# A Mamba-2 scan fused with a feed-forward layer: B and C turned by VectorE in place of TensorE

## The chip, the cores and the metric

The kernel runs on one core of a Trainium2 chip. A core has five engines that each work through a queue of their own, in order: TensorE (PE in the profile; its weight loads, PEld, overlap its matmuls), VectorE (DVE), ScalarE (ACT), GpSimd (POOL) and SyncE (SP), which here issues nearly all DMA transfers. They wait for one another through semaphores. The metric is the device time of one execution in microseconds; less is better.

## What is computed

The reference first runs a state-space scan over a batch of 4 with 8 heads, 768 tokens, 32 channels and a state of 16. It works in chunks; for each chunk

```python
cum = np.cumsum(la, axis=-1)                       # la = log(a)
L = np.exp(cum[:, :, :, None] - cum[:, :, None, :]) * causal
CB = np.einsum('bhin,bhjn->bhij', Cc, Bc)          # scores
y_intra = np.einsum('bhij,bhjd->bhid', CB * L, xc)
y_inter = np.einsum('bhin,bhnd->bhid', Cc, state) * np.exp(cum)[:, :, :, None]
y[:, :, sl] = y_intra + y_inter
state = decay_full * state + sum_j(Bc[j] * xc[j] * decay_from_j)
```

and then a feed-forward layer on the 3072 x 256 result: `h = x @ w_in` (2048 wide), `g = elu(h)`, `out = g @ w_out`.

## The kernel before

**Blocks.** The 768 tokens of each batch entry are three blocks of 256, which gives 12 blocks, numbered 0 to 11 in the order in which they are worked on. A block has u = 0, 1 (halves of 128 tokens), each of v = 0, 1 (chunks of 64 tokens). Blocks 0 to 3 are handled one by one; from block 4 on they go in pairs (4, 5), (6, 7), (8, 9), (10, 11).

**What a block needs.** `load_bc` brings B and C, `load_x` brings x, `spread_cum` and `spread_exp` bring decays back from DRAM. In `load_bc` tokens lie on the partitions, and each DMA moves rows of 16 floats (64 bytes), one for each token and head. The scores are products over the state index, so B and C must lie with (head, state) on the partitions and tokens along the free dimension: they have to be turned. `turn` does this with four 128x128 transposes on TensorE (L374) into two PSUM tiles `ps_tb` and `ps_tc`. ScalarE copies the turned B into `bt` (L378). VectorE makes `ctm` from the turned C (L381): two copies of it, each with every other head masked out by `hmask2`. `turn_exp` makes `cts` (L389), C times the decay `ec`. `scaled` (L364) makes `sc`, B times a decay, from B as it was loaded, on GpSimd.

Then `scores` (L459, on TensorE) multiplies `bt` and `ctm`; `decay` and `decay_of` fill `L` by exponentials on ScalarE (L439) and cut it to the causal part on GpSimd (L444, once for each half of the heads and each chunk parity); `weigh` (L468, VectorE) multiplies scores and `L` into `M`; `sums`, `states` and `across` (L489, L504 to L511, L534) carry the state on; `inside` (L553) makes the block's output and ScalarE moves it to `yT`, the input of the feed-forward layer.

**The feed-forward layer** is most of TensorE's work. For blocks 0 to 3 it is `l1` (L583) and `l2` (L707), with `elu` between them: on ScalarE a negated relu (L596) and an exponential (L603), on VectorE the combination `g` (L605). For later pairs a scheme with fewer products and more additions is used, in rounds i = 0 to 7: `front`, `mid` and `back` (L655) make the first layer, with `p_copy` on ScalarE (L665) and `u_sum` and further sums on VectorE (L673, L674, L682, L689, L690); `second` makes the second layer (L759), with sums on VectorE and GpSimd (L750, L723, L727). In a round, `mid` writes over a PSUM half that `p_copy` has read, and the first product of `back` needs the sum of L682.

**Weights** come in 16 pieces of float64 words that are rounded to float32 on chip (L157 to L200, on ScalarE, VectorE and GpSimd) while the first blocks are worked on.

**Order.** The program turns automatic scheduling off: every engine executes in the order in which the Python code issues its instructions. Blocks 4 to 11 are prepared by `scan_ahead`, which is called at every half round and gives the turn of the pair's first block after half round 5 and of the second after half round 7. Scores follow in half round 9. Blocks 2 and 3 are turned by explicit calls, block 2 at step 5 of the twelve-step loop (its scores at step 7), block 3 in round 1 of `n == 2` (its scores in round 2). The DMA queue of SyncE is in order as well.

Of the kernel before, what the change touches and what calls it, by code (L numbers as in the profile page):

```python
# [10 lines left out]
F32 = mybir.dt.float32  # L11
U32 = mybir.dt.uint32
BF16 = mybir.dt.bfloat16
ALU = mybir.AluOpType
ACT = mybir.ActivationFunctionType

P = 128
Q = 64
BLK = 2 * P
# [9 lines left out]
def kernel(  # L29
# [27 lines left out]
    nc = tc.nc  # L57
    NB, NH, S, D = x.shape
    N = B.shape[-1]
# [4 lines left out]
    DM, DF = moe_w_in.shape  # L64
# [6 lines left out]
    raw = ctx.enter_context(tc.tile_pool(name="raw", bufs=3))  # L71
    att = ctx.enter_context(tc.tile_pool(name="att", bufs=2))
    ffn = ctx.enter_context(tc.tile_pool(name="ffn", bufs=2))
# [13 lines left out]
    for k in range(4):  # L87
        (nc.scalar if k % 2 else nc.sync).dma_start(
            out=la0[BH * k:BH * (k + 1)],
            in_=a.rearrange("b h (c s) -> (b h) c s", s=P)[:, 0:2, :])  # L90
# [5 lines left out]
    st = {}  # L96

    def place(n):

        return 2 * (n // (2 * NG)) + n % 2, n // 2 % NG  # L100
# [5 lines left out]
    def load_bc(n, c_queue=nc.sync):  # L106
        b, g = place(n)
        st.setdefault(n, {})["bc"] = raw.tile([P, 2, 2, NH, N], F32, tag="bc", name="bc", bufs=2)
        for u in range(2):
            sl = slice((2 * g + u) * P, (2 * g + u + 1) * P)  # L110
            for k, src in enumerate((B, C)):
                (nc.sync, c_queue)[k].dma_start(  # L112
                    out=st[n]["bc"][:, k, u], in_=src[b, :, sl, :].rearrange("h s n -> s h n"))
# [118 lines left out]
    for v in range(2):  # L232
        nc.gpsimd.affine_select(
            out=low16[Q * v:Q * v + Q], in_=low16[Q * v:Q * v + Q], pattern=[[1, Q]],
# [5 lines left out]
        out=hmask, in_=hmask, pattern=[[-N, NH]], compare_op=ALU.is_ge, fill=0.0,  # L240
        base=0, channel_multiplier=1)
    nc.gpsimd.affine_select(
        out=hmask, in_=hmask, pattern=[[N, NH]], compare_op=ALU.is_ge, fill=0.0,
# [3 lines left out]
    hmask2 = const.tile([P, 2], F32, name="hmask2")  # L247
# [4 lines left out]
        out=minus, in0=ident, scalar1=-1.0, scalar2=None, op0=ALU.mult)  # L252
# [106 lines left out]
    def scaled(n, eng):  # L359

        s = st[n]
        s["sc"] = sc = att.tile([P, 2, NH, N], F32, tag="sc", name="sc", bufs=3)
        factor = eb0[:, :, NH * n:NH * (n + 1)] if n < 2 else eb[:, :, rows_of(n)]
        eng.tensor_tensor(  # L364
            out=sc, in0=s["bc"][:, 0],
            in1=factor.unsqueeze(3).to_broadcast([P, 2, NH, N]), op=ALU.mult)

    def turn(n):

        s = st[n]  # L370
        tb, tc_ = psum([P, 2, P], "ps_tb"), psum([P, 2, P], "ps_tc")
        for k, ps in enumerate((tb, tc_)):
            for u in range(2):
                nc.tensor.transpose(  # L374
                    out=ps[:, u], in_=s["bc"][:, k, u].rearrange("p h n -> p (h n)"),
                    identity=ident)
        s["bt"] = att.tile([P, 2, P], F32, tag="bt", name="bt", bufs=3)
        nc.scalar.copy(out=s["bt"], in_=tb)  # L378
        s["ct"] = tc_
        s["ctm"] = att.tile([P, 2, 2, P], F32, tag="ctm", name="ctm")  # L380
        nc.vector.tensor_tensor(  # L381
            out=s["ctm"], in0=tc_.unsqueeze(2).to_broadcast([P, 2, 2, P]),
            in1=hmask2.unsqueeze(1).unsqueeze(3).to_broadcast([P, 2, 2, P]), op=ALU.mult)

    def turn_exp(n):

        s = st[n]
        s["cts"] = att.tile([P, 2, P], F32, tag="cts", name="cts", bufs=3)
        nc.vector.tensor_tensor(out=s["cts"], in0=s.pop("ct"), in1=s["ec"], op=ALU.mult)  # L389

# [307 lines left out]
    def l2(n, j, half=None):  # L700


        if j == 0 and half != 1:
            o_of[n] = p_o.tile([P, 2, DM], F32, tag="o", name="ps_o")
        for m in (2 * j, 2 * j + 1) if half is None else (2 * j + half,):
            for ts in range(2):
                nc.tensor.matmul(  # L707
                    out=o_of[n][:, ts], lhsT=g_of[n, j][:, m % 2, ts * P:(ts + 1) * P],
                    rhs=w_out[:, m], start=(m == 0 and ts == 0), stop=(m == MC - 1),
                    skip_group_check=True)  # L710
        if j == MC // 2 - 1 and half != 0:
            ob = ffn.tile([P, 2, DM], F32, tag="ob", name="ob")
            nc.scalar.copy(out=ob, in_=o_of.pop(n))
            r0 = row_of(n)
            nc.sync.dma_start(
                out=out[r0:r0 + BLK, :].rearrange("(t p) e -> p t e", p=P), in_=ob)
# [197 lines left out]
    for s, (n, i) in enumerate((  # L914
            (1, 0), (1, 1), (1, 2), (0, 4), (1, 3), (0, 5), (1, 4), (0, 6), (1, 5), (0, 7),
            (1, 6), (1, 7))):
        l1(n, i)
        if s < 8:
            decay_of(2, s)
        if s == 7:  # L920
            scores(2)
            weigh(2, 0)
            weigh(2, 1)
        if s % 2 == 1 and todo < 10:
            w_take(todo, nc.vector)
            w_give(todo)
            w_load(todo + 6)
            todo += 1
        if s == 4:
            scaled(2, nc.gpsimd)  # L930
        if s == 5:
            turn(2)
            first_exp(2)
            turn_exp(2)
        if s == 8:
            spread_cum(3)
            load_x(3)
            spread_exp(3)
            weigh(2, 2)
            weigh(2, 3)  # L940

            st[0] = kept
            sums(2, 0, pool=p_o, tag="o", parts=(None, last))
            states(0, last)
            st.pop(0)
            states(2)
        if s == 10:
            spread_cum(4)
            inside(across(2), 2)
        if len(lag) > 1:  # L950
            elu()
# [15 lines left out]
    def scan_ahead(n, i):  # L967


        m = n + 2 + n % 2  # L970
        if 4 < m < NP and n % 2 == 1 and i in (4, 5):
            spread_cum(m + i - 4)
        m = n + 2 - n % 2
        if 4 <= m < NP and n % 2 == 0:
            if i < 2:
                load_bc(m + i)
                spread_exp(m + i)
            if i == 2:
                if m == 4:
                    spread_cum(5)  # L980
                load_x(m)
                load_x(m + 1)
            for k in (i,) if m == 4 else (i, i + 1) if i % 2 == 0 else ():
                if k >= 2:
                    decay(m + k // 6, (k - 2) % 4)
            if i in (5, 7):
                turn(m + i // 7)
                turn_exp(m + i // 7)
        if 4 <= m < NP and n % 2 == 1:
            if i == 0:  # L990
                scaled(m, nc.gpsimd)
                scaled(m + 1, nc.gpsimd)
            for k in (i,) if m == 4 else (i, i + 1) if i % 2 == 0 else ():
                if k < 2:
                    decay(m + 1, k + 2)
            if i == 2 and m == 4:
                scores(m, m + 1)
                sums(m, m + 1)
                for q in range(4):
                    weigh(m, q)  # L1000
                    weigh(m + 1, q)
                states(m)
                states(m + 1)
# [7 lines left out]
    for n in (2, 3):  # L1011
        for i in range(8):
            l2(n - 2, i)
            if todo < len(pieces):
                w_take(todo, nc.vector)
            end_of_two(n, 2 * i)
            l1(n, i)
            if todo < len(pieces):
                w_give(todo)
                w_load(todo + 6)  # L1020
                todo += 1
            while lag:
                elu()
            if n == 2:
                if i < 2:
                    decay(3, 2 * i)
                    decay(3, 2 * i + 1)
                if i == 1:
                    scaled(3, nc.gpsimd)
                    turn(3)  # L1030
                    turn_exp(3)
                if i == 2:
                    scores(3)
                    for q in range(4):
                        weigh(3, q)
                if i == 4:
                    sums(3)
                    states(3)
                if i == 6:
                    inside(across(3), 3)  # L1040
            else:
                if i == 0:
                    s_in[:], s_out[:] = weight_sums(), weight_sums()
                elif i < 7:
                    more_sums(i - 1)
            scan_ahead(n, i)
            end_of_two(n, 2 * i + 1)
    sum_t2(2, 0)
    left = (step for i in (6, 7) for step in weight_steps(nc.vector, a_out, s_out, i))

    for n in range(4, NP, 2):
        m = n + 2 if n + 2 < NP else None
# [13 lines left out]
        for k in range(16):  # L1066
            i = k // 2
# [54 lines left out]
    n = NP - 2  # L1122
# [41 lines left out]
```

## Time and profile before

| what | value |
|---|---|
| time, median of 3 (lowest, highest) | 364.5 us (363.97, 365.75) |
| span of the profiled execution | 362.9 us |
| transposes of B and C on PE (L374) | 48, mean of one 275 and 273 ns |
| bt on ACT (L378), 12 | mean 358 ns |
| ctm on DVE (L381), 12 | mean 682 ns |
| cts on DVE (L389), 12 | mean 414 ns |
| packets of DMA, of these under 512 B | 96,239, 77,312 |

A mean duration is from an instruction's start to its end; instructions of one engine overlap at their edges, so what one costs its engine is rather the distance to the start of the next. "Idle before" of an engine counts only for the engine that sets the end of a stretch. The chain of waits follows the last instruction back to what released it, step by step; in it one sees which engine that is.

### The profile page before, as it was taken

The page shows a single profiled execution, that of the slowest core. Times are in us where ns is not written, and L with a number is a line of the kernel's source. Part 1 is how long each engine was busy: PE and PEld are TensorE (multiplying, and loading weights), DVE is VectorE, ACT ScalarE, POOL GpSimd, SP SyncE. Part 2 cuts the span into 40 slices and gives each one's busy share as a digit, 9 for nine tenths or more (in the row PEclk, how much of TensorE's full clock was granted, in tenths as well). Part 3 has the DMA queues.
Part 4 walks back from the last instruction along what each step waited for, and adds up shares of the span by engine and source line. Part 5 has one row for each costly group of instructions (what it writes and reads, how often), then busy time and mean ns, then how long its engine had stood idle before and what let it go on. Part 6 is the DMA issues. An engine that isn't in the chain of part 4 may idle for free.

```text
span 362.9 us, 10146 instructions
## 1 busy us (share of the span) xinstructions
PE 354.3 (98%) x3978; PEld 316.9 (87%) x3978; DVE 242.2 (67%) x547; ACT 200.7 (55%) x499; POOL 227.1 (63%) x366
## 2 busy tenths in 40 slices
PE   8899999999999999999999999999999999999996
PEld 5578778888888998898999998999989999999995
DVE  4989887972697668784567684666685666666212
ACT  4858969767435567635485735386735352534100
POOL 4454443663567896679457578567587555456893
PEclk9999999999999999999999999999999999999999
DMA  8877995563050560053530045540000100000001
GB/s 155 203 203 147 240 308 141 66 116 63 3 116 19 65 85 12 4 115 48 96 65 2 3 95 68 93 72 0 3 2 4 58 2 0 3 0 32 29 2 58
DMA packets 96239, 25.33 MB, mean 70 GB/s; under 512 B 77312, under 2 KB 92096, under 8 KB 96192
## 3 DMA queue, kind: packets, MB, share of 16 engines
q1 hardware_dynamic: 94016, 24.49, 33.0%
q8 instruction: 31, 0.51, 0.6%
q10 hardware_dynamic: 2176, 0.20, 0.4%
q14 instruction: 16, 0.13, 0.1%
HBM read 21.33 MB, written 3.34 MB: 68 GB/s over the span
## 4 chain that ended last, share of the span: by engine, by line
PE 81%; DVE 7%; ACT 3%; DMA 3%; SPq 2%; issue 2%; POOL 1%; ACTq 0%; DVEq 0%
PE ps_o L759 32%; PE ps_h L655 25%; PE ps_h L583 10%; PE ps_o L707 8%; SPq L112 2%; PE ps_g L459 1%; DMA w<-in_moe_w_in_dram 1%; DVE g L605 1%; PE ps_y L553 1%; ACT e L596 1%; PE ps_st L489 1%; ACT e L603 1%; DMA flat<-F 1%; DVE mag L183 1%; PE ps_y L534 1%
## 5 line engine op out<-in xcount | busy, mean ns | idle before, releaser
L596 ACT ACTIVATE e<-ps_h 128x512 f32<-128x512 f32 x96 | 56.5, 588 | 93.1 <-DVE ps_h L689 71.2
L605 DVE SCALAR_TENSOR_TENSOR g<-e,ps_h 128x512 f32<-128x512 f32 x96 | 65.3, 681 | 39.2 <-ACT e L603 35.8
L759 PEld LDWEIGHTS ps_o<-w_out,g 128*128 128x128 f32 x640 | 80.3, 192 | 3.3 <-issue 0.5
L759 PE MATMUL ps_o<-w_out,g 128*128 128x128 f32 x640 | 81.4, 275 | 0.0
L727 POOL TENSOR_TENSOR g<-g 128x256 f32<-128x256 f32 x34 | 24.8, 729 | 67.1 <-DVE g L605 67.1
L583 PE MATMUL ps_h<-yT,w_in 128*128 128x256 f32 x256 | 60.6, 383 | 2.5 <-POOL w_in L200 1.8
L603 ACT ACTIVATE e<-e 128x512 f32<-128x512 f32 x96 | 60.9, 634 | 2.2
L583 PEld LDWEIGHTS ps_h<-yT,w_in 128*128 128x128 f32 x256 | 47.8, 190 | 10.6 <-POOL w_in L200 2.8
L759 PE MATMUL ps_o<-w_sum,g 128*128 128x128 f32 x320 | 43.0, 275 | 0.0
L759 PEld LDWEIGHTS ps_o<-w_sum,g 128*128 128x128 f32 x320 | 41.1, 192 | 1.4
L439 ACT ACTIVATE L<-L,ncum 128x64 f32<-128x64 f32 x160 | 41.0, 338 | 0.0
L655 PE MATMUL ps_h<-y_sum,w_in 128*128 128x256 f32 x128 | 38.6, 383 | 0.7 <-DVE ps_h L682 0.7
L655 PE MATMUL ps_h<-y_sum,w_sum 128*128 128x256 f32 x128 | 38.5, 382 | 0.5 <-DVE g L605 0.5
L655 PE MATMUL ps_h<-yT,w_in 128*128 128x256 f32 x128 | 38.8, 385 | 0.0
L444 POOL TENSOR_SCALAR_AFFINE_SELECT L<-L 64x512 f32<-64x512 f32 x40 | 27.3, 682 | 13.1 <-ACT L L439 11.8
L707 PE MATMUL ps_o<-w_out,g 128*128 128x256 f32 x128 | 30.8, 383 | 0.0
L655 PEld LDWEIGHTS ps_h<-y_sum,w_sum 128*128 128x128 f32 x128 | 23.9, 190 | 5.3 <-DVE g L605 1.3
L723 POOL TENSOR_TENSOR g<-t,g 128x256 f32<-128x256 f32 x40 | 27.9, 729 | 0.8 <-PE ps_o L759 0.8
L723 POOL TENSOR_TENSOR t<-g 128x256 f32<-128x256 f32 x40 | 28.1, 736 | 0.2
L723 POOL TENSOR_TENSOR g<-g,t 128x256 f32<-128x256 f32 x40 | 27.9, 730 | 0.2
L707 PEld LDWEIGHTS ps_o<-w_out,g 128*128 128x128 f32 x128 | 23.7, 190 | 3.4 <-POOL L L444 0.2
L689 DVE TENSOR_TENSOR ps_h<-ps_h,u_sum 128x256 f32<-128x256 f32 x32 | 13.7, 429 | 18.3 <-PE ps_h L655 18.3
(109 smaller groups left out, 538.3 us busy)
## 6 DMA issues: line engine op xcount, KB each, us to landing
L<-flat SPq DMA_DIRECT2D x20, 256.0 KB, 5.3
w<-in_moe_w_in_dram SPq DMA_DIRECT2D x8, 512.0 KB, 5.2
w<-in_moe_w_out_dram SPq DMA_DIRECT2D x8, 512.0 KB, 6.1
xr<-in_x_dram SPq DMA_DIRECT2D x24, 128.0 KB, 3.4
out_dram<-c_sum SPq DMA_DIRECT2D x10, 256.0 KB, 2.1
bc<-in_B_dram SPq DMA_DIRECT2D x24, 64.0 KB, 4.4
bc<-in_C_dram SPq DMA_DIRECT2D x22, 64.0 KB, 3.4
ec<-flat_exp SPq DMA_DIRECT2D x72, 16.0 KB, 1.7
```

Source lines behind the costliest of these rows:

```text
L439: nc.scalar.activation(L[:, h, u], L[:, h, u], ACT.Exp, bias=ncum[:, u, row:row + 1])
L444: nc.gpsimd.affine_select(out=part, in_=part, pattern=[[0, 4], [0, 2], [1, Q]], compare_op=ALU.is_ge, fill=0.0, base=0, channel_multiplier=-1)
L583: nc.tensor.matmul(out=ps[:, j], lhsT=w_in[:, k, m * P:(m + 1) * P], rhs=yT[n // 2][:, k, n % 2].rearrange("p u i -> p (u i)"), start=(k = ...
L596: nc.scalar.activation(begun[0], lag[0][2], ACT.Relu, scale=-1.0)
L603: nc.scalar.activation(e, e, ACT.Exp, scale=-1.0)
L605: nc.vector.scalar_tensor_tensor(out=g_of[n, i], in0=e, scalar=1.0, in1=ps, op0=ALU.subtract, op1=ALU.max)
L655: nc.tensor.matmul(out=out, lhsT=lhsT, rhs=rhs, start=first, stop=True, skip_group_check=True)
L689: nc.vector.tensor_tensor(out=c1[:, 1], in0=c1[:, 1], in1=u[:, 0], op=ALU.add)
L707: nc.tensor.matmul(out=o_of[n][:, ts], lhsT=g_of[n, j][:, m % 2, ts * P:(ts + 1) * P], rhs=w_out[:, m], start=(m == 0 and ts == 0), stop=( ...
L723: nc.gpsimd.tensor_tensor(out=out, in0=in0, in1=in1, op=ALU.subtract)
L727: eng.tensor_tensor(out=b12, in0=b12, in1=g_of[n, i][:, 0], op=ALU.subtract)
L759: nc.tensor.matmul(out=ps[:, ts], lhsT=b[:, ts * P:(ts + 1) * P], rhs=a[:, i], start=(i == chunk[0] and ts == 0), stop=(i == chunk[-1]), s ...
```

## The change

For blocks 2 to 11, B and C are loaded in another arrangement: 8 consecutive tokens of one head are 128 floats, 512 contiguous bytes. One DMA takes every other head (four heads of 32 such groups, which are the 128 partitions), and two fill a tile whose free dimension is (head parity, 8 tokens, 16 states). For each of the 8 tokens, head parity and state give 32 columns, and with 32 partitions a square, which VectorE turns in place of TensorE: one transpose instruction for B, one for C, 8 x 4 squares each. The result `bct` has (head, state) on the partitions as before, but in SBUF and not in PSUM. Since `sc` needs B with tokens on the partitions, B is also loaded as before, into `b_tok`.

`turn_squares` takes the place of `turn` and `turn_exp`. What makes `ctm` and `cts` is an argument: both on GpSimd for block 2; `ctm` on GpSimd and `cts` on VectorE for block 3; for blocks 4 to 11 `ctm` on ScalarE, as two instructions, and `cts` on VectorE. The copy `bt` is no longer needed. `bct` has two buffers (`bt` had three), and the output tile `ob` has one in place of two.

The purpose is to relieve TensorE of 40 of the 48 transposes.

```diff
     def load_bc(n, c_queue=nc.sync):
...
+        if n > 1:
+            st[n]["b"] = raw.tile([P, 2, NH, N], F32, tag="b", name="b_tok", bufs=2)
+            for u in range(2):
+                sl = slice((2 * g + u) * P, (2 * g + u + 1) * P)
+                nc.sync.dma_start(
+                    out=st[n]["b"][:, u], in_=B[b, :, sl, :].rearrange("h s n -> s h n"))
...
+            squares = st[n]["bc"].rearrange("p k u h n -> p k (u h n)").rearrange(
+                "p k (m r) -> p k m r", m=2)
+            for k, src in enumerate((B, C)):
+                for m in range(2):
+                    nc.sync.dma_start(
+                        out=squares[:, k, m],
+                        in_=src[b, m:NH:2, g * BLK:(g + 1) * BLK, :].rearrange(
+                            "q (c t) n -> q c (t n)", t=8))
+            return
...
-            out=sc, in0=s["bc"][:, 0],
+            out=sc, in0=s["b"] if n > 1 else s["bc"][:, 0],
...
-        s["bt"] = att.tile([P, 2, P], F32, tag="bt", name="bt", bufs=3)
+        s["bt"] = att.tile([P, 2, 2, P], F32, tag="bct", name="bct", bufs=2)[:, 0]
...
+    def turn_squares(n, mask, eng):
...
+        t = att.tile([P, 2, 2, P], F32, tag="bct", name="bct", bufs=2)
+        squares = s["bc"].rearrange("p k u h n -> p k (u h n)").rearrange(
+            "p k (m t n) -> p k t m n", m=2, n=N)
+        for k in range(2):
+            nc.vector.transpose(
+                out=t[:, k].rearrange("p u i -> p (u i)").rearrange("p (c t) -> p t c", t=8),
+                in_=squares[:, k])
+        s["bt"], ct = t[:, 0], t[:, 1]
+        s["ctm"] = att.tile([P, 2, 2, P], F32, tag="ctm", name="ctm")
+        if mask is nc.scalar:
+            for k in range(2):
+                mask.activation(s["ctm"][:, :, k], ct, ACT.Copy, scale=hmask2[:, k:k + 1])
+        else:
+            mask.tensor_tensor(
+                out=s["ctm"], in0=ct.unsqueeze(2).to_broadcast([P, 2, 2, P]),
+                in1=hmask2.unsqueeze(1).unsqueeze(3).to_broadcast([P, 2, 2, P]), op=ALU.mult)
+        s["cts"] = att.tile([P, 2, P], F32, tag="cts", name="cts", bufs=3)
+        eng.tensor_tensor(out=s["cts"], in0=ct, in1=s["ec"], op=ALU.mult)
...
-            ob = ffn.tile([P, 2, DM], F32, tag="ob", name="ob")
+            ob = ffn.tile([P, 2, DM], F32, tag="ob", name="ob", bufs=1)
...
-            turn(2)
             first_exp(2)
-            turn_exp(2)
+            turn_squares(2, nc.gpsimd, nc.gpsimd)
...
-                turn(m + i // 7)
-                turn_exp(m + i // 7)
+                turn_squares(m + i // 7, nc.scalar, nc.vector)
...
-                    turn(3)
-                    turn_exp(3)
+                    turn_squares(3, nc.gpsimd, nc.vector)
```

## The prediction

> **What bounds the kernel now.** I read the page first: busy shares, then the chain that ended last.
>
> ```profile
> PE 354.3 (98%) x3978; PEld 316.9 (87%) x3978; DVE 242.2 (67%) x547; ACT 200.7 (55%) x499; POOL 227.1 (63%) x366
> ...
> PE 81%; DVE 7%; ACT 3%; DMA 3%; SPq 2%; issue 2%; POOL 1%; ACTq 0%; DVEq 0%
> ```
>
> TensorE is busy for 98% of the span and makes up 81% of the chain. A busy PE need not be a PE at its peak, so I followed the chain in order of time: from 43.8 us on it is almost wholly matmuls that follow one another with no gap. So from there an instruction taken off PE is worth its place in the chain, and an instruction that makes PE wait costs the whole wait. What the transposes hold is read from the chain between 185 and 202 us:
>
> ```profile
> 192.27 0.44 PE ps_o L759 x4
> 192.71 0.22 PE ps_tb L374 x2
> 192.93 0.22 PE ps_tc L374 x2
> 193.15 1.30 PE ps_h L655 x6
> ```
>
> The groups give 275 ns as the mean of one transpose, but they are pipelined: the four of a block hold the chain for 0.22 + 0.22 = **0.44 us**. Then I read the timeline, all engines, at the places where block 3 and blocks 6 to 11 are turned.
>
> Block 3 (start, duration, engine, line):
>
> ```profile
> 61.99 2.01 ACT L439 ACTIVATE L<-L,ncum 128x64 f32<-128x64 f32 x8
> ...
> 64.07 1.58 POOL L444 TENSOR_SCALAR_AFFINE_SELECT L<-L 64x512 f32<-64x512 f32 x2 [0.19 <-ACT L L439]
> ...
> 64.43 0.69 PE L459 MATMUL ps_g<-ctm,bt 32*64 32x128 f32 x32
> ...
> 65.05 1.99 PE L707 MATMUL ps_o<-w_out,g 128*128 128x256 f32 x8
> ...
> 65.73 0.69 POOL L364 TENSOR_TENSOR sc<-bc,eb 128x256 f32<-128x256 f32 x1
> ```
>
> scores(3) runs at 64.43 while GpSimd has yet to do two causal selects and the scaling. Block 8:
>
> ```profile
> 193.93 0.69 DVE L605 SCALAR_TENSOR_TENSOR g<-e,ps_h 128x512 f32<-128x512 f32 x1 [0.99 <-ACT e L603]
> ...
> 194.53 0.39 ACT L665 COPY p_copy<-ps_h 128x256 f32<-128x256 f32 x1
> 194.54 0.68 DVE L381 TENSOR_TENSOR ctm<-ps_tc,hmask 128x512 f32<-128x512 f32 x1
> ...
> 195.47 0.41 DVE L673 TENSOR_TENSOR u_sum<-ps_h,p_copy 128x256 f32<-128x256 f32 x1
> ...
> 196.07 0.60 PE L655 MATMUL ps_h<-yT,w_in 128*128 128x256 f32 x2
> ...
> 197.18 0.42 DVE L682 TENSOR_TENSOR ps_h<-ps_h,u_sum 128x256 f32<-128x256 f32 x1
> ...
> 197.82 0.60 PE L655 MATMUL ps_h<-y_sum,w_in 128*128 128x256 f32 x2
> ```
>
> L682 ends at 197.60, and PE's next product, which waits for it, starts at 197.82: some 0.2 us of slack.
>
> [...] the same 128x128 difference of L631 took 0.28 us at 137.38 and 0.71 us at 137.69, when GpSimd was busy. cts becomes such an instruction.
>
> **The change, part by part.**
>
> *PE.* 40 transposes go, four in each of ten blocks. By the chain, 10 x 0.44 = 4.4 us, the whole possible gain.
>
> *Price of a VectorE transpose.* The nearest row is cts, also 256 elements in one pass: 0.41 us, the next instruction starting 0.33 after it (195.14, 195.47). I take these. The low end is 0.28 (L183 on 128x256), the high end 0.8 (two passes). Two transposes and cts then take 0.33 x 3 = 1.0 us of VectorE, where ctm and cts took 195.47 - 194.54 = 0.93: nothing for VectorE itself.
>
> *Block 3.* In the new order GpSimd does both selects, sc, then ctm, and PE's scores(3) wait for ctm. The decays on ACT end at 64.00 (the 61.99 line), the selects at 65.65, sc at 66.42. ctm of 128x512 on GpSimd: L200 takes 1.27 for that size; bounds are 1.1 (from sc and L511: 0.655 us for 256 elements, 0.303 for 64, continued to 512) and 1.46 (two L723). So ctm ends at 67.7, and scores follow at 67.75 instead of 64.43. After their 0.62 us PE goes on at 68.3 instead of 65.05: **+3.2 us**. It stands still here; everything queued behind the scores on PE is late, and the chain has nothing later that could absorb it (PE's listed waits after 60 us sum to 1.2 us). VectorE waits there too, with the M products, but without harm to PE.
>
> *Block 2.* GpSimd gets ctm (1.27) and cts (0.73) between w_sum, which ends at 42.52, and the selects. ctm ends at 43.8, scores run until 44.5, and the L583 matmuls start then instead of at 43.81: +0.65. Against this, C is no longer fetched in 64-byte pieces: 2,048 of the block's 4,096 small packets go for 512 of 512 bytes, in the stretch where one issue of L112 was held 4.30 us and the weight piece behind it landed at 35.14, with ScalarE idle 1.1 us for it. If that comes 1.1 us sooner, ctm is ready at 42.7 and 0.4 is gained. I take **+0.1**, from -0.4 to +0.65.
>
> *Blocks 4 and 5.* ctm goes to ScalarE, which was idle 1.43 us soon after (at 88.97); scores come only at 95.84. Nothing waits: 2 x -0.44 = **-0.9**.
>
> *Blocks 6, 8, 10 (the first turn of each pair).* ScalarE now does ctm in two instructions, which wait for VectorE's second transpose; behind them in its queue stand p_copy and the next exp. By block 8: g starts at 193.93, the transposes at 194.54 and 194.87, the second ends at 195.28. ctm starts at 195.32 and 195.59, p_copy at 195.86 (spacing 0.27, about that of bt to p_copy), ending at 196.25. u_sum (L673) waits for p_copy: 196.29 instead of 195.47, **0.82 late**. Behind it on VectorE are L674, g, an addition and L682, all as late; L682 ends at 198.43. PE's product starts 0.06 later (as at 142.20, after L682 ended at 142.14), so at 198.49 instead of 197.82: +0.67. The 0.44 that PE saved is lost in this wait. Block 10 has the same slack (L682 ends at 253.27, the product starts at 253.49): +0.67. Block 6 had none, for PE already waits 0.67 there: +0.82. Together **+2.2**.
>
> *Blocks 7, 9, 11.* The same delay, but L682 had stood idle 0.50 for PE. At 199.1: u_sum 202.57 instead of 201.75, L682 ends at 204.39, the product starts at 204.45 instead of 204.41. The gain is cancelled: **+0.1** for three.
>
> *At no cost:* the two extra DMA issues of a block (loads are issued 8 us or more before the turn, as at 178 against 192); the single ob buffer (its two users are at 84.55 and 116.49); bct with two buffers (scores(4) end at 97, block 6 is turned at 135); bt's copies, which leave ScalarE, and cts's contention, which ends before u_sum may start.
>
> Sum: 0.1 + 3.2 - 0.9 + 2.2 + 0.1 = +4.7, so 364.5 + 4.7 = **369.2 us**.
>
> **The rivals.** (1) *PE's 4.4 us are simply gained*: 360.1. For it: 98% busy, 67% VectorE. Against it: GpSimd's order at block 3, where only a much earlier ctm would do. (2) *Only block 3 waits*: ScalarE's delay is absorbed, six blocks gain 0.44 each: 0.1 + 3.2 - 0.9 - 2.6 = -0.2, so 364.3. For it: ScalarE is busy 55%. Against it: its queue is in order and p_copy stands right behind ctm. (3) *The transposes take 0.8 each* and start 0.7 apart: u_sum is another 0.8 late in all six blocks, all of it on PE: 6 x 0.8 = 4.8, so 374.0.
>
> **How the numbers follow.** My forecast 0.64, rival (1) 0.12, rival (2) 0.14, rival (3) 0.10. Within the forecast, block 2 (-0.5 to +0.55), ctm's 1.1 to 1.46 on GpSimd and a transpose of 0.28 (0.25 off each of the six blocks, -1.5) give 367 to 370. The range reaches down to rival (2), 364.0, and up to 373, nearly to rival (3); rival (1) and the end of (3) stay out. Faster by over 0.5% (below 362.7): 0.13. Within 0.5%: 0.14. Slower (above 366.3): 0.73.
>
> **What would show it.** In the profile after: PE's scores(3) wait for GpSimd's ctm some 3 us near 64 to 68; u_sum at blocks 6 to 11 starts behind p_copy and not behind cts; PE's wait for L682 grows from 0.7 to some 2 us or more; 40 fewer matmuls. Wrong it would be if ctm(3) on GpSimd comes before 65 us, if StreamTranspose takes well under 0.28, or if PE's products after a turn start as early as without the two ScalarE instructions.

## The result, and the profile after

| | before | after |
|---|---|---|
| time, median (lowest to highest) | 364.5 us (363.97 to 365.75) | 380.5 us (378.73 to 382.92) |
| ratio, 95% interval | | 1.0447 (1.0401 to 1.0493) |
| span of the profiled execution | 362.9 us | 377.0 us |

The change makes the kernel 16.0 us slower. 369.2 was forecast, with a range up to 373.0: the direction was right, the size was not. The profile after belongs to the fastest of its four runs (378.73 us), so it has to explain 14.1 us; the others showed a TensorE clock that was as low or lower (0.982 to 0.995 on the mean).

The page after, engines and chain:

```profile
PE 353.3 (94%) x3938; PEld 315.5 (84%) x3938; DVE 248.5 (66%) x556; ACT 205.1 (54%) x505; POOL 229.8 (61%) x369
...
PE 66%; POOL 10%; DVE 9%; ACT 6%; issue 5%; DMA 2%; SPq 1%; DVEq 0%; ACTq 0%; POOLq 0%
```

The 40 transposes are gone (3978 matmuls became 3938), but PE's busy time fell by 1.0 us only, and its share of the chain from 81% to 66%: PE now waits for others. For whom is told by PE's waits after (engine, its line, engine and line waited for: us in total, times, longest):

```profile
PE ps_h L695 <- ACT p_copy L705: 7.2, 6, 2.3
PE ps_g L499 <- POOL ctm L425: 5.3, 2, 3.6
PE ps_y L593 <- issue: 2.4, 2, 1.5
...
PE ps_st L529 <- POOL sc L381: 0.9, 3, 0.3
PE ps_h L695 <- DVE ps_h L722: 0.3, 2, 0.2
```

In the kernel after, the lines stand 40 further down (L655 is L695, L665 is L705, L682 is L722); the new ones are L416 (VectorE's transpose), L423 (`ctm` on ScalarE), L425 (`ctm` on GpSimd) and L429 (`cts`). The waits for `p_copy` and for `ctm` are new. So is a wait of PE inside the block's output (L593) for nothing that the profile names.

Where each delay arises is read by laying the n-th VectorE instruction that writes `g` (L605, then L645) in one trace beside the n-th in the other; below this is called the `g` method. The delay of after grows as follows, in us:

| stretch | delay gained | forecast |
|---|---|---|
| block 2 | +0.5 | +0.1 |
| block 3 | +2.8 | +3.2 |
| blocks 4, 5 | -0.7 | -0.9 |
| blocks 6, 7 | +3.8 | +0.8 |
| blocks 8, 9 | +2.5 | +0.7 |
| PE's gap at 231 us | +0.5 | none |
| near 250 us | +0.4 | none |
| blocks 10, 11 | +2.4 | +0.7 |
| PE's gap at 286 us | +1.7 | none |
| rest | +0.2 | none |

**Block 3** in the timeline after (start, duration, engine, line, operation; in brackets the idle time before it and what ended it):

```profile
65.80 0.68 POOL L381 TENSOR_TENSOR sc<-b_tok,eb 128x256 f32<-128x256 f32 x1
66.45 1.22 POOL L425 TENSOR_TENSOR ctm<-bct,hmask 128x512 f32<-128x512 f32 x1
67.72 0.70 PE L499 MATMUL ps_g<-ctm,bct 32*64 32x128 f32 x32 [3.59 <-POOL ctm L425]
68.20 1.07 ACT L479 ACTIVATE L<-L,ncum 128x64 f32<-128x64 f32 x4 [2.31 <-DMA L<-flat]
68.35 2.00 PE L747 MATMUL ps_o<-w_out,g 128*128 128x256 f32 x8
```

GpSimd comes to `ctm` at 66.45, behind `sc`, and PE's scores start at 67.72 (forecast 67.75). PE goes on at 68.35 instead of 65.05.

**Block 8** in the timeline after:

```profile
200.28 0.69 DVE L645 SCALAR_TENSOR_TENSOR g<-e,ps_h 128x512 f32<-128x512 f32 x1 [0.99 <-ACT e L643]
200.88 1.12 DVE L416 STREAM_TRANSPOSE bct<-bc 128x256 f32<-128x256 f32 x2
202.03 0.91 ACT L423 ACTIVATE ctm<-bct,hmask 128x256 f32<-128x256 f32 x2 [1.30 <-DVE bct L416]
202.84 0.35 ACT L705 COPY p_copy<-ps_h 128x256 f32<-128x256 f32 x1
203.22 0.42 DVE L713 TENSOR_TENSOR u_sum<-ps_h,p_copy 128x256 f32<-128x256 f32 x1 [0.77 <-ACT p_copy L705]
203.24 0.70 PE L695 MATMUL ps_h<-yT,w_in 128*128 128x256 f32 x2 [1.10 <-ACT p_copy L705]
204.95 0.42 DVE L722 TENSOR_TENSOR ps_h<-ps_h,u_sum 128x256 f32<-128x256 f32 x1
205.43 0.70 PE L695 MATMUL ps_h<-y_sum,w_in 128*128 128x256 f32 x2 [0.16 <-DVE ps_h L722]
```

This is the queue that the prediction described: transposes, the two `ctm` behind the second, `p_copy` behind them. Read it against `g`: `p_copy` ends 2.91 us after `g` starts (202.84 + 0.35 - 200.28); the prediction had 2.32. Both of PE's products that depend on it are late: the one that writes where `p_copy` reads, which starts 2.96 after `g` instead of 2.14, and the one that waits for L722, 5.15 instead of 3.89.

**TensorE's clock.** After the wait of 2.31 us in block 6 the clock falls. Stretches of after (start and end, length, busy time and count of PE, PEld, DVE, ACT and POOL, granted PE clock, DMA share, GB/s), first the one with this wait and the next, then those around block 3's wait:

```profile
141.03:144.44 3.41, 1.10 (x8) 0.88 (x8) 2.58 (x6) 2.12 (x6) 1.91 (x3) 1.00 0.00 0
144.44:147.85 3.41, 3.41 (x14) 3.06 (x13) 1.71 (x4) 1.94 (x9) 2.05 (x3) 0.50 0.02 5
62.51:65.93 3.42, 1.63 (x8) 1.10 (x6) 3.39 (x7) 3.35 (x11) 2.80 (x4) 1.00 0.96 264
65.93:69.34 3.41, 1.62 (x37) 1.35 (x38) 3.38 (x6) 1.14 (x5) 2.32 (x3) 1.00 0.75 111
69.34:72.75 3.41, 3.41 (x17) 3.02 (x16) 2.96 (x8) 1.12 (x3) 1.03 (x2) 1.00 0.34 81
```

PE stands for 2.31 of the first 3.41 us, and then works for 3.41 us at half the clock; a busy share of 100% conceals that. Half of 3.41 is 1.7 us, but by the `g` method blocks 6 and 7 lose only 1.3 more than blocks 8 and 9 (3.8 against 2.5); by the author's estimate part of the slow work fills time in which PE would have waited for VectorE. Block 3's wait is longer, 3.59 us, and no fall follows it.

These stretches are not chosen at will. In each of the twelve traces all changes of the granted clock lie whole multiples of 3.41 us apart (in after they are at 144.44, 147.85 and 376.54, in late_mask at 46.26, 49.68, 70.16, 76.98, 288.61 and 292.02), and the stretches above are those of that grid. Block 3's wait lies across a border, with 1.79 us of idle PE on either side. The longest PE wait of the kernel before after 20 us is this one, and its clock doesn't fall there:

```profile
PE ps_h L655 <- DVE ps_h L682: 0.7, 1, 0.7
```

### The profile page after: what moved, and what is told of

Its sections match the earlier page's. It is cut to its first block, busy times and chain, and to the rows that moved or that the text cites. A ratio compares the mean times of both kernels' runs of the same rounds, so it can differ in the third digit from the quotient of the medians.

```text
span 377.0 us, 10110 instructions
## 1 busy us (share of the span) xinstructions
PE 353.3 (94%) x3938; PEld 315.5 (84%) x3938; DVE 248.5 (66%) x556; ACT 205.1 (54%) x505; POOL 229.8 (61%) x369
## 4 chain that ended last, share of the span: by engine, by line
PE 66%; POOL 10%; DVE 9%; ACT 6%; issue 5%; DMA 2%; SPq 1%; DVEq 0%; ACTq 0%; POOLq 0%
PE ps_o L799 25%; PE ps_h L695 20%; PE ps_h L623 8%; PE ps_o L747 7%; POOL g L763 3%; PE ps_y L593 2%; DVE bct L416 2%; ACT e L636 2%; ACT e L643 2%; DMA w<-in_moe_w_in_dram 1%; POOL sc L381 1%; DVE mag L207 1%; PE ps_y L574 1%; DVE g L645 1%; SPq L121 1%
## 5 line engine op out<-in xcount | busy, mean ns | idle before, releaser
L645 DVE SCALAR_TENSOR_TENSOR g<-e,ps_h 128x512 f32<-128x512 f32 x96 | 65.5, 683 | 38.0 <-ACT e L643 34.5
L623 PEld LDWEIGHTS ps_h<-yT,w_in 128*128 128x128 f32 x256 | 48.0, 190 | 9.7 <-POOL w_in L217 3.0
L695 PE MATMUL ps_h<-yT,w_in 128*128 128x256 f32 x128 | 39.5, 390 | 7.2 <-ACT p_copy L705 7.2
L799 PE MATMUL ps_o<-w_sum,g 128*128 128x128 f32 x320 | 43.9, 279 | 0.0
L799 PEld LDWEIGHTS ps_o<-w_sum,g 128*128 128x128 f32 x320 | 42.0, 196 | 1.5
L695 PE MATMUL ps_h<-y_sum,w_in 128*128 128x256 f32 x128 | 39.2, 389 | 0.3 <-DVE ps_h L722 0.3
L695 PE MATMUL ps_h<-y_sum,w_sum 128*128 128x256 f32 x128 | 38.7, 384 | 0.0
L695 PEld LDWEIGHTS ps_h<-y_sum,w_sum 128*128 128x128 f32 x128 | 24.4, 192 | 3.6 <-DVE g L645 0.3
L695 PEld LDWEIGHTS ps_h<-yT,w_in 128*128 128x128 f32 x128 | 19.7, 191 | 9.0 <-ACT p_copy L705 8.4
```

Of the source, the lines that this page charges most:

```text
L623: nc.tensor.matmul(out=ps[:, j], lhsT=w_in[:, k, m * P:(m + 1) * P], rhs=yT[n // 2][:, k, n % 2].rearrange("p u i -> p (u i)"), start=(k = ...
L645: nc.vector.scalar_tensor_tensor(out=g_of[n, i], in0=e, scalar=1.0, in1=ps, op0=ALU.subtract, op1=ALU.max)
L695: nc.tensor.matmul(out=out, lhsT=lhsT, rhs=rhs, start=first, stop=True, skip_group_check=True)
L799: nc.tensor.matmul(out=ps[:, ts], lhsT=b[:, ts * P:(ts + 1) * P], rhs=a[:, i], start=(i == chunk[0] and ts == 0), stop=(i == chunk[-1]), s ...
```

## Experiments

Each is a kernel of its own, timed beside the kernel before on the same chip; the ratio is to that one. The diffs are against the kernel after unless another is named. Theories: **order** (GpSimd's order costs some 3 us at block 3, ScalarE's `ctm` ahead of `p_copy` the most in blocks 6 to 11), against **an early wait is made good later**, and against **another engine than ScalarE** as what PE waits for in the late blocks.

### 1 and 2: the change by halves

Squares for blocks 2 and 3 alone (only23), and for blocks 4 to 11 alone (only411):

```diff
-        if n > 1:
+        if 1 < n < 4:          # only23; only411: if n > 3
...
-                turn_squares(m + i // 7, nc.scalar, nc.vector)
+                turn(m + i // 7)          # only23; only411 does this for blocks 2 and 3
+                turn_exp(m + i // 7)
```

> Squares only for blocks 2 and 3, all others turned by TensorE as before. Theory (waits in the queues, block by block): only the two waits of PE for ctm on GpSimd are there; the changed kernel's trace puts them at +2.9 us by the end of block 3, so 367.4 us (366.8 to 368.2), with PE waiting some 3.6 us for ctm once and none of PE's waits for p_copy. Rival (every block turned by VectorE costs about the same, 14 us over ten blocks): 1.4 us for each, so 367.3 us as well, but with no single long wait. Rival (the early wait is made good later, as VectorE and ScalarE gain time during it): under 365.5 us.

> Squares only for blocks 4 to 11, blocks 2 and 3 turned by TensorE as before. Theory (waits block by block, additive): the changed kernel's +14.2 less the +2.9 of blocks 2 and 3, so about 375.8 us (374.5 to 378). Rival (the wait at block 3 throws the later rounds out of step, and without it they would hide the masks): about 361 us.

Measured: only23 369.98 us (369.38 to 371.11) against 364.12, ratio 1.0155 (1.012 to 1.019), +5.9; only411 373.97 (372.62 to 375.85), ratio 1.0249 (1.02 to 1.0297), +9.9. Together +15.7, where the whole change cost 16.0: the halves add up, and nothing of the early wait is made good, for by the `g` method only23's delay stays at 4.5 from block 3 to the end. That rival falls. That the sum fits so closely is in part luck, for the parts differ: only23's trace has a fall of the clock after block 3 that after's has not, only411's lacks the gaps in L593, and its blocks 4 and 5 lose 1.7 where they gain 0.7 in after. only411 came out a little under its range; only23 costs 2.6 us more than its two waits were forecast to. PE's waits of only23, and the stretch of the clock's grid with the second of them, with the next:

```profile
PE ps_g L499 <- POOL ctm L425: 4.7, 2, 3.5
```

```profile
63.70:67.11 3.41, 0.30 (x2) 0.00 (x0) 3.38 (x5) 3.03 (x9) 3.08 (x5) 1.00 1.06 129
67.11:70.53 3.42, 3.07 (x37) 2.38 (x38) 3.38 (x8) 0.49 (x1) 1.56 (x2) 0.50 0.19 44
```

4.7 us of waiting (1.21 for block 2, 3.46 for block 3), and then the clock at 0.50 from 67.1 to 70.5 us, which loses 1.5 more: here 3.11 us of the wait of 3.46 lie in one stretch of the grid. In only411 the extra DMA issues showed up, in its timeline:

```profile
85.83 1.06 ACT L479 ACTIVATE L<-L,ncum 128x64 f32<-128x64 f32 x4 [1.66 <-DMA L<-flat]
86.80 0.56 ACT L753 COPY ob<-ps_o 128x512 f32<-128x512 f32 x1
87.41 1.99 PE L747 MATMUL ps_o<-w_out,g 128*128 128x256 f32 x8 [2.21 <-ACT ob L753]
```

A load of B and C is six issues on SyncE's queue instead of four. The `L` that stands behind them (block 5's) lands late, ScalarE waits 1.66 us for it, and PE 2.21 for the output copy behind that on ScalarE. In the kernel after it is block 4's `L` that lands late: the wait of 2.31 at 68.20 (block 3 above) lies beside PE's longer wait for `ctm` and costs little, and with PE late block 5's `L` is there in time.

### 3 and 4: what PE waits for in blocks 6 to 11

late_mask puts ScalarE's two `ctm` half a round later, behind `p_copy`; pool_mask gives them to GpSimd:

```diff
         if mask is nc.scalar:
-            for k in range(2):
-                mask.activation(s["ctm"][:, :, k], ct, ACT.Copy, scale=hmask2[:, k:k + 1])
+            s["ct"] = ct                  # late_mask: these two half a round later
...
-                turn_squares(m + i // 7, nc.scalar, nc.vector)
+                turn_squares(m + i // 7, nc.gpsimd, nc.vector)      # pool_mask
```

> The changed kernel with one edit: for blocks 4 to 11 the two ctm instructions stand half a round later in ScalarE's queue, behind p_copy, exp and the decays; same work on every engine. Theory (p_copy stands behind ctm, which stands behind the transposes): u_sum is late only by what the two transposes and cts take beyond ctm and cts, some 0.47 us, and PE mostly gets its 0.44 us back: blocks 2 and 3 +2.9, 4 and 5 -0.9, 6 to 11 about 0, so 366.5 us (365.5 to 369), and PE's wait for p_copy (8.4 us) is gone. Rival (the length of VectorE's transposes alone holds up the rounds, the order on ScalarE does not matter): over 375 us.

> The changed kernel with one edit: for blocks 4 to 11 ctm is made by GpSimd in one instruction and not by ScalarE in two. Theory (ScalarE's queue order): as with late_mask, 366 to 370 us, PE's wait for p_copy gone. Rival (VectorE's transposes alone): over 375 us. Second rival (the wait moves: ctm of 1.1 us in GpSimd's queue delays the differences of g that PE's second layer needs): over 372 us, with PE waiting for L763 or L767.

Measured: late_mask 376.44 us (375.6 to 380.47), ratio 1.0351 (1.0289 to 1.0413); pool_mask 375.06 (374.15 to 375.98), ratio 1.0291 (1.0256 to 1.0326). Both missed their forecast times. PE's waits of pool_mask:

```profile
PE ps_g L499 <- POOL ctm L425: 4.7, 2, 3.5
PE ps_h L695 <- DVE ps_h L722: 3.2, 3, 1.5
PE ps_y L593 <- issue: 2.7, 3, 1.7
```

Those of late_mask (its lines stand 5 further down):

```profile
PE ps_g L504 <- POOL ctm L424: 6.4, 2, 3.5
PE ps_h L700 <- DVE ps_h L727: 3.2, 3, 1.5
PE ps_y L598 <- issue: 2.1, 2, 1.7
```

The wait for `p_copy` is gone in both (7.2 us in after's list, where late_mask's expectation has 8.4), so ScalarE's order was its cause. By the `g` method a pair now costs +0.78, +0.75 and +0.69 in pool_mask, against 2.5 on the mean in after (1.3 of clock taken off). ScalarE's place in the queue is worth some 1.7 us a pair. The rest is put down to VectorE, which experiments 6 and 7 test: PE waits for L722, which stands behind the transposes. Without any delay a pair would have gained 2 x 0.44 = 0.88, so VectorE's part takes 0.75 + 0.88 = 1.6 us a pair. No wait of PE for GpSimd's sums took its place.

Why the times missed: the early waits cost as before, with the clock at half after block 3, and near 280 us another 3.4 us is lost in a gap of PE (1.73) and a half clock behind it (half of 3.41). Late_mask's profile, its slowest run, had worse: 0.50 from 46.26 to 49.68, from 70.16 to 76.98 and from 288.61 to 292.02 us, 13.65 us at half clock.

### 5: the gap that no wait explains

Pool_mask's gap in its timeline:

```profile
283.59 0.96 PE L593 MATMUL ps_y<-M,xr 64*32 64x64 f32 x47 [1.73 <-issue]
```

In after there is one of 0.91 us at 231 and one of 1.50 at 286. They were seen in after, late_mask and pool_mask, which have 3938 matmuls, not in only23 (3970), only411 (3946) and before (3978). Idea: the gap belongs to a place in PE's instruction stream. pe_pad is pool_mask with eight tiny matmuls at the start (sixteen in the page's count, 3954):

```diff
     idle_product(3)
+    for _ in range(8):
+        nc.tensor.matmul(
+            out=ps_idle[:, 0, 0:2], lhsT=idle, rhs=idle[:, 0:2], start=True, stop=True)
```

> pool_mask with eight matmuls of 2 columns added on TensorE right at the start, where it waits for the first loads; nothing else. In the profiles of the changed kernel, late_mask and pool_mask, which have the same TensorE instruction stream, PE stands 1.5 to 1.7 us in the middle of the inside products (L593) of blocks 10 and 11, for nothing that the profile shows, in pool_mask with its clock halved for some 3 us after it; in only411, whose stream is 8 matmuls longer there, it does not. Theory (the gap belongs to the position in TensorE's instruction stream): with 8 matmuls more it is gone from that place or moves, and the time falls from 375.1 by 2 to 3.5 us to 371.5 to 373 us. Rival (the gap has to do with what the other engines do there): it stays, 375 us.

Measured: 376.47 us (373.7 to 377.69) against 365.21, ratio 1.0282 (1.0224 to 1.0339). The gaps at 228 and 281 us are gone, as the idea says, but another has come near the start, in pe_pad's timeline:

```profile
14.93 0.43 PE L596 MATMUL ps_y<-M,xr 64*32 64x64 f32 x6 [2.10 <-issue]
```

So the gap moves with the instruction stream, and no time was won. It sits each time among the many small products of L593 (L596 here).

The traces show more than this experiment does. Number all of PE's instructions in a trace from 0, weight loads and semaphore instructions included. Each of the 17 such gaps of over 0.3 us after the first 10 us, in eight kernels, stands before an instruction whose number leaves 193 or 194 when divided by 256: 5313 and 6593 in after, 4033, 5314 and 6594 in pool_mask, 450 in pe_pad. Every page lists a queue of kind "instruction" (queue, kind, packets, MB, share), here that of after:

```profile
q8 instruction: 31, 0.51, 0.6%
```

These are 31 packets of 16,384 bytes, for 7,961 PE instructions in after's trace: one for every 256 or so. Each of the gaps ends 1.2 to 1.6 us after such a packet has landed; in pool_mask the one before the gap above lands at 282.13, and PE goes on at 283.59. What PE waits for there was not shown: no view names it and no run tests it.

### 6: what a transpose costs

t_shape is pool_mask with other patterns of the transpose: the output contiguous for odd blocks, input and output for even ones. It leaves the turned values in other places, so that what follows computes on displaced B and C.

```diff
-                out=t[:, k].rearrange("p u i -> p (u i)").rearrange("p (c t) -> p t c", t=8),
-                in_=squares[:, k])
+                out=flat_t.rearrange("p (t c) -> p t c", t=8) if n % 2 else flat_t,
+                in_=squares[:, k] if n % 2 else s["bc"][:, k].rearrange("p u h n -> p (u h n)"))
```

> pool_mask with the transposes' access patterns changed, so that the turned values land in other places: for even blocks input and output both run through the 256 elements contiguously, for odd blocks only the output. Looked at for the duration of one transpose alone (0.63 us before, 0.50 us from start to start of two). Theory (the strides cost the time): about 0.42 us, as cts. Rival (a transpose of 256 fp32 elements takes that long whatever the pattern): 0.63 us in all.

The transposes by tile, first after, then t_shape (count: shortest/median/longest ns, first and last start):

```profile
L416 DVE STREAM_TRANSPOSE bct<-bc x20: 609/632/648, 41.1 to 268.0; 128x256 f32<-128x256 f32 x20
L423 ACT ACTIVATE ctm<-bct,hmask x16: 491/500/508, 82.6 to 269.1; 128x256 f32<-128x256 f32 x16
```

```profile
L417 DVE STREAM_TRANSPOSE bct<-bc x20: 397/418/439, 42.1 to 262.9; 128x256 f32<-128x256 f32 x20
```

0.418 us in both forms, against 0.632: the pattern of the output, where neighbours of a square are 8 floats apart, costs 0.21 us each; that of the input costs nothing that shows in the 0.397 to 0.439 us of the two forms. A turn's two transposes take 0.76 us together, start to end, in place of 1.11. This is also a test of VectorE's part: with 0.35 us less in each turn, the pairs from block 6 on cost +0.45, +0.05 and 0.0 by the `g` method, where pool_mask's cost +0.78, +0.75 and +0.69. The single run took 372.73.

### 7: the turn where VectorE is idle

In pool_mask VectorE turns while L713 to L722 are urgent. Between L722 and L729 it stands idle for PE anyway: in the kernel before 0.85 us at block 8, ahead of L689 (L729 in after):

```profile
198.46 0.43 DVE L689 TENSOR_TENSOR ps_h<-ps_h,u_sum 128x256 f32<-128x256 f32 x1 [0.85 <-PE ps_h L655]
```

gap_turn is pool_mask with the turns of blocks 6 to 11 put there, and `cts` on GpSimd too:

```diff
-            if i in (5, 7):
-                turn_squares(m + i // 7, nc.scalar, nc.vector)
+            if i in (5, 7) and m == 4:
+                turn_squares(m + i // 7, nc.gpsimd, nc.vector)
...
                 mid(n, i)
+                if m and k in (5, 7):
+                    turn_squares(m + k // 7, nc.gpsimd, nc.gpsimd)
```

> pool_mask with the turn of blocks 6 to 11 at another place: the two transposes stand in VectorE's queue between L722 (the sum after mid) and L729 (after back), where VectorE stood idle 0.8 to 0.9 us for PE, and cts is made by GpSimd too. Theory (what is left in pool_mask, some +0.75 us in each pair, is the transposes' 1.1 us ahead of u_sum): the pairs gain up to 0.9 us each, so 375.1 - 5 = 370 us (369 to 372). Rival (the transposes now hold up L729, and by it relu and the next round): 374 us or more.

Measured: 369.33 us (368.66 to 369.64), ratio 1.0095 (1.0062 to 1.0127), as forecast. The pairs now gain: the delay falls from 5.03 to 3.82, 4.35 to 3.49 and 3.51 to 2.65. Two things were moved, the transposes and `cts`; which of them brings how much is not separated. Of pool_mask's 3.2 us of waits for L722 this is left:

```profile
PE ps_h L695 <- DVE ps_h L722: 0.2, 1, 0.2
```

### 8: squares only where they pay

best_1 is the kernel before with squares for blocks 6 to 11 alone, placed as in gap_turn:

```diff
+        if n > 5:
+            st[n]["b"] = raw.tile([P, 2, NH, N], F32, tag="b", name="b_tok", bufs=2)
...
-            if i in (5, 7):
+            if i in (5, 7) and m == 4:
                 turn(m + i // 7)
                 turn_exp(m + i // 7)
...
+                if m and k in (5, 7):
+                    turn_squares(m + k // 7, nc.gpsimd, nc.gpsimd)
```

> The kernel before with squares only for blocks 6 to 11, turned as in gap_turn (transposes between L722 and L729, ctm and cts on GpSimd); blocks 2 to 5 as before. Theory (no early waits, and the transposes in a gap of VectorE): six blocks gain 0.44 us each, 364.1 - 2.6 = 361.5 us (360.8 to 363). Rival (GpSimd's extra 1.9 us a block delay the differences of g for PE): 364 us or more. If the gap of PE inside L593 comes up here, 2 to 3 us more.

Measured: 361.81 us (361.26 to 362.76), ratio **0.9892 (0.9851 to 0.9933)**: faster than before. Between the traces 2.68 us are won by the `g` method, and 24 transposes by the prediction's price are 6 x 0.44 = 2.64. By pairs it is 1.2, 0.87 and 0.87, against 0.88 for two blocks; in the first pair PE's wait of 0.67 in the kernel before is gone as well, and 0.2 had been lost ahead of it. The page of best_1, and VectorE around block 8 in its timeline:

```profile
PE 351.8 (98%) x3954; PEld 314.4 (87%) x3954; DVE 242.9 (67%) x547; ACT 199.9 (55%) x493; POOL 237.4 (66%) x378
```

```profile
195.74 0.42 DVE L722 TENSOR_TENSOR ps_h<-ps_h,u_sum 128x256 f32<-128x256 f32 x1
196.07 1.10 DVE L416 STREAM_TRANSPOSE bct<-bc 128x256 f32<-128x256 f32 x2
196.30 0.30 PEld L695 LDWEIGHTS ps_h<-y_sum,w_in 128*128 128x128 f32 x2
196.41 0.60 PE L695 MATMUL ps_h<-y_sum,w_in 128*128 128x256 f32 x2
196.63 0.41 PEld L695 LDWEIGHTS ps_h<-yT,w_sum 128*128 128x128 f32 x2
196.84 0.59 PE L695 MATMUL ps_h<-yT,w_sum 128*128 128x256 f32 x2
197.04 0.45 DVE L729 TENSOR_TENSOR ps_h<-ps_h,u_sum 128x256 f32<-128x256 f32 x1
```

VectorE's 1.10 us of transposes lie beside PE's products, and L729 starts 1.30 us after L722, where it was 1.28 in the kernel before (198.46 - 197.18). PE is busy for 98% again, and no wait of PE after the start is new.

### 9 and 10: can the early blocks be had too?

early_3 is gap_turn with block 3's transposes and `ctm` one round earlier, so that GpSimd does `ctm` ahead of the selects. best_2 is best_1 with squares for blocks 4 and 5 as well, and `spread_cum(5)` issued ahead of `load_bc(5)`:

```diff
             if n == 2:
+                if i == 0:
+                    turn_squares(3, nc.gpsimd, None)     # early_3
...
+                if i == 1 and m == 4:
+                    spread_cum(5)                        # best_2
                 load_bc(m + i)
```

> gap_turn with block 3 turned one round earlier: its two transposes on VectorE and its ctm on GpSimd stand in round 0 of n == 2, ahead of the causal selects and of the scaling; its cts stays in round 1. Theory (scores of block 3 wait only because ctm stands last of four in GpSimd's queue): PE's 3.5 us wait is gone, and with it the stretch of halved TensorE clock that follows it in gap_turn (68 to 72 us, about 1.9 us): 369.3 - 3.3 - 1.9 = 364.1 us (363.3 to 366). Rival (GpSimd and VectorE have no room there, and something else waits in its place): over 367 us.

> best_1 with squares for blocks 4 and 5 as well, their ctm on GpSimd, and the decays of block 5 (L from flat) issued ahead of the loads of B and C of block 5 and not behind them. Theory (in only411 blocks 4 and 5 lost their gain because SyncE's queue, with six loads a block where four were, brought L of block 5 late, for which ScalarE and, behind it, the output copy and PE waited): two more gains of 0.44, so 360.9 us, 0.25% under best_1. Rival (the extra loads still come late, or VectorE has no room there): 362 us or more.

early_3 missed: 370.08 us (367.25 to 370.39) against 365.33, ratio 1.0115 (1.008 to 1.0149), no better than gap_turn. In its profile, that of its fastest run, the wait for `ctm` of block 3 is gone, with the fall of the clock that followed it; what comes instead is, in the timeline:

```profile
86.11 1.06 ACT L485 ACTIVATE L<-L,ncum 128x64 f32<-128x64 f32 x4 [1.84 <-DMA L<-flat]
87.08 0.56 ACT L759 COPY ob<-ps_o 128x512 f32<-128x512 f32 x1
87.69 1.56 PE L753 MATMUL ps_o<-w_out,g 128*128 128x256 f32 x6 [1.36 <-ACT ob L759]
```

That is only411's wait again: once PE no longer stands at block 3, the late `L` is uncovered. Block 2 still waits 2.05, and three gaps of 0.72, 0.68 and 1.92 remain. What made its other runs 3 us slower than the profiled one wasn't profiled; their mean clocks, 0.989 to 0.995 against 1.000, say that the clock fell in them.

best_2: 361.86 us (360.09 to 362.46), ratio 0.9902 (0.9877 to 0.9928). Its trace is 3.2 us shorter than that of before, but its time can't be told from best_1's.

## Why the prediction was right or wrong

- **Price of PE's transposes, 0.44 us a block: right.** best_1 took away six blocks' worth with no new wait of PE, and won 2.68; its last two pairs gained 0.87 each, where 2 x 0.44 is 0.88.
- **Block 3, +3.2: right**, by its own chain of selects, `sc` and `ctm` (1.22 us, taken 1.27); its times, 67.75 + 0.62 against 65.05, give 3.3, and PE was 3.3 late. No half clock followed in this trace; in only23's it did, for 1.5 us more. **Block 2, +0.1: too low**; +0.5 was inside the stated bounds: as if the gain from fewer packets had not come. **Blocks 4 and 5, -0.9: right** but for 0.2 in after, though not alone, as only411 shows.
- **Blocks 6 to 11, +2.3: wrong, 8.7 measured.** The step is "Price of a VectorE transpose", and with it the spacing of `ctm`. 0.33 from start to start was taken and 0.49 measured (0.632 long), for the row it was taken from, `cts`, writes contiguously: into a contiguous output the transpose took 0.418 in t_shape, and the stride of its output costs the other 0.21. The two `ctm` were spaced by 0.27, from a copy; 0.41 was measured. In sum `p_copy` ends 2.91 us after `g` and not 2.32: 0.59 late in each of six blocks, 3.5 us. Of the 0.59, 0.37 are the transposes (the second ends 1.72 after `g` and not 1.35), and most of the rest is the spacing of `ctm`.
- **Blocks 7, 9, 11 at +0.1** rested on slack of 0.5 at L682. With the real sizes PE doesn't come that far: it waits earlier, for `p_copy`, in the product that writes where `p_copy` reads. The prediction followed only `u_sum` to L682. So its sign to look for, a wait for L682 of 2 us, was wrong: that is 0.3 in after, and the wait for `p_copy` 7.2. Block 9 loses 0.90 by the `g` method, where the prediction's +0.04 with `p_copy` 0.59 later would give 0.63; in three blocks this path is worth some 0.8. After these turns PE's sums wait for `sc`, 0.9 in all on the list, 0.7 by the `g` method.
- These, 3.5, 0.8 and 0.7, and the clock's 1.3 account for 6.3 of the 6.4 us missed in the six blocks. The sum is worked out, not measured by itself; that ScalarE's order and VectorE's transposes are the two sources is shown by late_mask, pool_mask, t_shape and gap_turn. The whole miss is 11.3 us: 6.4 here, 2.2 in the gaps, 0.4 near 250 us, some 0.4 in all other stretches together, and 1.8 between the profiled run and the median.
- **"At no cost", the DMA issues: wrong.** The prediction looked at when the turn needs these loads, not at what stands behind them in the queue. only411 and early_3 show PE waits of 2.21 and 1.36 for that; in after itself they are covered.
- **`cts` longer beside a busy GpSimd: right.** The two L631 that the prediction sets side by side are a bad pair (the second is a sum written in place, and GpSimd was busy from 137.44), but over its 32 instructions on VectorE the reading holds on the whole: the seven with GpSimd wholly idle took 0.28 to 0.29 us, and of the other 25 four took 0.28 to 0.29 and the rest 0.41 to 0.77. In after, `cts` took 0.87 to 0.92 in the three blocks (3, 4 and 5) where GpSimd was busy for most of it, and 0.42 to 0.44 in blocks 6 to 11, where it was idle for most or all of it. In before, where `cts` reads the turned C from PSUM, it took 0.41 to 0.42 in all twelve blocks, with GpSimd idle or busy.
- **Not in the prediction at all:** the clock at half after a wait, and the gaps in L593 (0.5 and 1.7 by `g`).
- **The rivals.** Rival (3), transposes of 0.8 that delay `u_sum` in all six blocks, 374.0, was nearest in size, in part by luck: it is right that the transposes take longer and that all six blocks pay, but at 0.5 they are only part of it. Rivals (1) and (2) fell: in these runs blocks 6 to 11 gain only where both `ctm` and the turn are moved, as in gap_turn.
- **Open:** the 0.4 us near 250 us; the 1.8 us by which the median is above the profiled run (two of the other three runs had mean clocks of 0.990 and 0.982 against 0.995, and by an estimate one fall of 3.41 us lowers the mean by 0.0045, half of 3.41 in a span of 377.0); and a test of what causes the gaps.

## What to carry to other kernels

An engine with a third of its time free is free only in certain places: look for the idle stretch in its own timeline (here 0.85 us between L722 and L729) and put the new work there, not ahead of an instruction that the bounding engine waits for. Price a new instruction with the access pattern that it will have, its output's stride too (here 0.63 us against 0.42), and follow every reader of what is delayed, not only the longest chain. On an engine that hardly stood still before, a new wait may cost more than its own length (in only23 3.46 us, and 1.5 more by the clock), so moving only the part of the work that brings no wait (best_1) can beat moving more. And a gap without a releaser is worth a look at the numbers of the instructions and at the instruction queue.

## What the runs showed of the hardware

- A VectorE transpose of 128x256 float32 took 0.42 us into contiguous output (t_shape) and 0.63 into output 32 bytes apart (after).
- In all twelve traces the changes of TensorE's granted clock lie whole multiples of 3.41 us apart, and each stretch of half clock before the end lasted 3.41 or 6.83 us. On this grid, from the first stretch at full clock to 20 us before the end, PE is idle for 2.07 to 3.36 us in ten stretches, and half a clock followed all ten. Of those with 1.40 to 1.79 us it followed six: four with 1.40 or 1.41 near 14 us, and two with 1.72 and 1.73 around a gap amid small products. It did not follow the two of 1.79, one of 1.71 and seven of 1.45 to 1.60. Of after's 3.59 at block 3, 1.79 us lie on either side of a border, and the clock stayed at 1.00; of only23's 3.46, 3.11 idle us lie in one stretch, and 3.41 us at 0.50 followed. No run moves one and the same wait across a border.
- TensorE stood for up to 2.10 us (pe_pad) amid small products with no wait that the profile names. All six kernels with 3938 matmuls had such gaps of 0.5 us or more late in the run; of the others only best_2 had one there, of 0.47. The 17 over 0.3 us stand at instruction numbers of 193 or 194 modulo 256, 1.2 to 1.6 us after an instruction packet of 16,384 bytes landed.
